# One core of block-sparse attention and a feed-forward: the written order of all engines replaced by another search's order

## The chip, the cores and the metric

The program runs on one core of one Trainium2 chip. The metric is device time in microseconds (us). The kernel before takes 261.37 us, the median of 3 runs (261.06 to 262.38).

A core has engines that run side by side, each through its own list of instructions in order: TensorE (PE in the profile; its weight loads are PEld), VectorE (DVE), ScalarE (ACT), GpSimd (POOL) and SyncE (SP), which here only starts transfers. An engine waits at an instruction until semaphores tell it that the data are there and the buffer is free. So the order in which each list is written decides who stands behind whom.

## The reference, cut to what matters

```python
# attention: batch 4, 8 heads, 768 positions, head_dim 64, blocks of 32
scores = scale * np.matmul(q, k.transpose(0, 1, 3, 2))
mask = np.abs(blk_i - blk_j) <= 1
mask = mask | (blk_i == 0) | (blk_j == 0) | (blk_i == n_blocks - 1) | (blk_j == n_blocks - 1)
# ... and three sampled key blocks for each block of queries
scores = np.where(mask, scores, -1000000000.0)
attn = softmax(scores)                 # row maximum taken off, exp, divided by the sum
x = np.matmul(attn, v)                 # to (3072 tokens, 512)
# feed-forward: 512 -> 2048 -> 512
h = x @ w_in
g = h * (1.0 / (1.0 + np.exp(-beta * h)))
out = g @ w_out
```

All inputs and the output are float32; the kernel multiplies in float16.

## The kernel before, in words

**Tiles.** Two heads of one batch make a pair; there are 16 pairs (x = 0 to 15). For each pair, keys and queries are loaded (`st`), cast to float16 (`s16`), transposed to `kX` and `qX` (the buffers `set`), and the values are cast into `va`. For the first four pairs the transposes run on TensorE (`turn`) with a copy out of PSUM behind each (`turn cp`); for later pairs they are transfers from SyncE's queue. A pair is worked in two tiles of queries, 256 and 512 wide.

**One attention tile.** Six scoring steps (`sc`, TensorE, into a double bank of PSUM), six exponentials (`ex`, ScalarE, out `et`), six multiplications by the mask (`mk`, VectorE), then the product with the values (`av`, TensorE, one step per head), the reciprocal of the sums and the scaling (`norm`, VectorE, out `xst`), and a transpose into `x`: on TensorE with a copy (`x turn`, `x cp`) for the first tiles, afterwards as a transfer (`x<-xst`). For the first six tiles the mask is not multiplied: TensorE adds it to the scores with a second product (`onehot`), so these `sc` are twice as long and there is no `mk`.

**The feed-forward.** Over groups of 256 or 512 tokens: `hp` (x by w_in, TensorE), `th` (tanh, ScalarE), `gm` (VectorE), then the product with w_out: plain (`op`) for the first group, and for the others a scheme of seven half-size products (`pr`) with sums of `g` (`sg`) and of `w_out` (`tw`) on VectorE. `cv` takes the product out of PSUM into `osb`, on ScalarE or VectorE; `osb` is then stored.

**Row tiles.** `sc` uses 64 of the array's 128 rows per product, so two heads run side by side. Some 128-row steps are written in halves and paired ("`118P1:119`" says that step 118 and step 119 alternate, half by half; `in_halves`), so that they can stand beside `sc` without a change between 64 and 128 rows.

**The order.** The steps are numbered 0 to 1298 by the order in which the program creates them. The string `STEPS` (line 43 on) holds the order of emission and all placements: `31S4` is step 31 on SP with buffer slot 4; letters P, A, D, G, S are TensorE, ScalarE, VectorE, GpSimd and SyncE. `in_steps` (line 164) reads it and sets each step's engine and slots; the loop at the end of the kernel function emits the steps in that order. Each engine's list is the subsequence with its letter. A cast on GpSimd also waits for the VectorE step emitted last before it (line 1056, "beside PSUM readers"). The loads of the first keys of pairs 1 and 0 (steps 27 and 13) are issued at the very start from ScalarE's queue, whatever their place in the string.

**Steps that the prediction names.**

| steps | what |
|---|---|
| 27, 35, 28, 36, 29, 37, 30, 38 | keys of pair 1 (first third, rest): loads, casts, turns, copies |
| 31, 32, 33, 34 | queries of pair 1: load, cast, turn, copy |
| 0, 1, 2, 3; 4 to 9 | the mask: block table, product, the shut form, its copy; three products with three copies (4 and 5, 6 and 7, 8 and 9) |
| 13 to 24 | keys and queries of pair 0 (14, 18, 22 casts; 15, 19, 23 turns; 16, 20, 24 copies) |
| 41 to 48 | keys and queries of pair 2 (42, 46 casts; 43, 47 turns; 44, 48 copies) |
| 26, 40, 50, 60 | casts of the values of pairs 0, 1, 2, 3 |
| 51 to 58 | keys and queries of pair 3 |
| 88, 92, 90; 80, 76, 78; 104, 100, 102 | first scoring steps of pairs 1, 0 and 2 |
| 94 | the first step of product with the values |
| 70 to 72, 73 to 75 | loads of w_in and w_out on GpSimd's queue |
| 172 to 181 | first group's product with w_out (`op`); 175 and 181 are its last quarters |
| 340 to 347 | sums of w_out (`tw`) |
| 480, 705, 894 | transposes of x by transfer, the last of their group; 481, 706, 930, 906 the `hp` behind them |

Of the kernel before, what the change touches and what calls it, by code (L numbers as in the profile page):

```python
# [47 lines left out]
112P1 103A6 26D1 49S6 94P0 95P 113A7 82P2 83P 96D1 97D1 116P0 84Da 185A0 114P1 117Ac 190P3 66D0  # L48
85D0 191A8 59S7 60G2 50D0 106P2 107P 108Da 109D2 115Ab 188P0 86P6 67P7 189Ad 87D1 68D 186P2
118P1:119 202P3 119P 187A9 194P0 120Dh 121D3 203A1 192P2 11P2 110P3 98P6 122P7 12D 111D 193A4  # L50
195A2 204P1 123D 99D 205A3 124P5 145P4 125A2 139P7 142P0 133P6 146A0 143A3 134A1 136P2 127P1 140A5
130P3 126D0 147D 212P2 137A6 128A2 131A4 144D 135D 141D 213A5 138D 132D 206P3 207A6 151P2 157P3
163P4 154P5 158A0 164A1 129D 155A4 152A5 159D 210P3 196P0 211Ae 165D 156D 153D 208P2 228P1 197P
209Aa 198D0 220S4 221D5 199D3 169P6 229A7 166P7 223S8 170A0 160P4 148P5 167A6 161A3 149A2 234P1
# [6 lines left out]
390P1 393P3 310P4 394A5 292P1 391A8 293A0 313P7 295P0 314A2 343D 389D 386D 346D 311A4 296A3 395D
347D 392D 301P5 302A6 298P6 405G3 227G3 412P1 294D0 315D 312D 303D 299A5 325P17:307 418P2 410S5
413A0 300D 398D 297D 307P 415P1 408G0 288G5 289S 411G1 291G2 383D 419A2 308A5 309D 326A6 327D
304P6 305A1 316P0 416A3 317A2 319P7 320A0 306D 414D 318D 417D 321D 334P5 335A1 421P1 422A7 328P1
329A6 322P0 323A0 427P3 336D 348D0 330D 324D 331P23:337 428Ab 424P2 425A1 337P 400P0:399 435P3
399P 429D 420D 426D 423D 438P2 338A1 332A5 401D8 402D0 436A4 441P3 439Ae 333D 430P0:431 440D 339D
447P2 431P 442Ac 448Aa 437D 444P3 450P1 445A0 357P4 406S2 409S 470P3 354P5:358 451A1 464P1 471A5
358P 432D9 433D3 351D 458P0 461P3 465A8 467P1 459Ad 468A2 446D 452D 355P 449D 462A6 352D 443D 349D
453P0 454P 568P1 466D 356D0 359D 473P3 455Dc 456D1 569A9 365P:362 565P0 469D 474A3 472D 570D 460D
463D 475D 576P1 566Ae 362P 363P:366 577Aa 403S2 177S 590S4 593S1 591G2 601P3 562P0 602A7 366P 361D  # L70
477P1:476 364D 604P3 476P 360D 353D 563Ab 367A1 598P0 478D3 479D2 371P 605A0 350D 582P3 599A8
583A2 623P1 368P:372 624A6 620P0 626P3 372P 579P1 369P 596S5 434S 612S2 615S8 618S7 634S6 621A1
637S0 457S 640S3 578D 594D0 613D4 584D 567D 373D 592S0 480S 580A5 627A4 481P0 482A6 499P1 564D
625D 370D 638G5 616G6 635G2 487P2 500A0 595S 571P3 572P 488A1 483D1 501D 642P0 489D 614S2 656S4
659S1 374P3:490 484P24:496 600D 573D4 636S1 657G4 660G3 643A9 617S 658S3 639S 377S 661S 378S 645P0
646Ac 490P 491A5 606D 574D0 575S1 622D 644D 619D3 492D 581D 648P3 496P 649A3 485A1 486D 508P0
509A5 510D 493P1 520P3 497A6 521A0 494A2 375P 376A 502P0 628D 503A3 522D 498D 495D 504D 603D 529D0
670P1 664P3 671Ad 511P5 512A1 517P4 513D 607P1 608P 597G2 665Ab 666D 609D1 610D3 647D 518A6 681P0
682Ae 678P3 526P5 683D 585P1 586P 587D5 588D4 505P0 527A3 679A8 692P1 519D 528D 667P3 506A4 514P1
693A0 629P2 523P2 630P 515A0 507D 650D 516D 631D0 632D0 651P0:652 668A7 684P3 524A5 525D 652P  # L80
653Dc 685Aa 641G0 532D 654D2 790P2 791A1 535P23:538 698P3 796P0 538P 539P:536 802P2 672D 686D 530D
533D 797A6 699A2 536P 803A5 537A0 669D 680D 695P0 787P3 540D 673P2 674P 675Dc 676D1 543P 696Ac
788A7 810P2 799P0 662S2 688P3:687 546P:544 800Ab 663G1 798D 694D 531D 700D 633S 380S 379S 833S6
836S4 839S8 687P 813P0 689Df 690D0 544P 811Ad 841P2 847P3 814A4 655S 534D 589S 864S0 793P0 834G0
842A9 545A 547P 848A3 677S 691S 611S 697D 701P2 702P 542D 794A0 548A1 815D 703D0 704D2 549P 550P
801D 865D5 541D 551D 705S 844P3 825P0 822P2 823A8 826Aa 845Ae 552P 553P 555P 706P0 709P1 812D 795D
792D 789D 804D 554D 837G3 707A1 710A3 708D0 711D 730P3 819P2 731A2 806P3:805 824D 732D 843D 820A2
816P0 817Ac 805P 853P2 739P3:556 872P0 807D4 808D3 867S0 870S1 895S3 898S6 866S0 849D 818D 850P3
868G1 901S7 821D 556P 854A0 715P45:712 557D 851A5 740A3 856P3 873A1 857A6 871G2 896G2 741D 852D
874D 712P 716A2 717D 827D 713A1 835S2 558S 561S 721P23:727 878P0 875P3 879A7 727P 724P4 828P0 855D  # L90
714D 876Ab 722A6 858D 899G6 560S 838S 897S1 559S 809S0 900S 869S 728A3 725A4 742P5 751P7 718P6
743A0 877D 723D 829P 726D 729D 744D 830D1 881P1 831D2 719A5 752A3 745P45:733 846D 753D 882A2 884P0
733P 885A4 734A2 746A0 720D 736P23:748 987P0 754D0 735D 747D 988A8 748P 737A3 860P3:859 738D 749A6
984P0 887P2 859P 888Aa 750D 996P1 861D7 883D 862D0 760P45:763 985Ac 1038P0 990P3 763P 764P:761
997A5 991A0 886D 757D 880D 755D 889D 759D 1039Ad 1027P1 761P 890P0:891 1018P3 1028A3 762A1 758D
765D 891P 892D6 1019A9 893D1 768P:771 1021P1 993P3 1022A6 994Ae 1015P0 771P 772P:769 1007S1 1010S5
832S 1016A1 1030P1 999P3 863S 1000A2 1031A4 902G3 840D0 766D 1011D3 769P 894S 930P1 903P7 931A2
933P3 915P0 909P2 904A1 770A 756D 767D 998D 986D 1008D6 924P6 934A5 910A4 1009S3 1013S5 1012S
1001D 989D 995D 1017D 905D1 918P7 774P 932D 773A0 921P1 935D 1032D 911D 916A2 925A0 919A3 912P3
917D 992D 920D 775P 776D 926D 906P2 777P 922A6 923D 913A0 907A1 914D 908D 1014D1 1029D 1003P3:1002  # L100
1061P0 1062A7 780P:778 1047P1 1002P 1041P0 1004Dg 1005D0 778P 1048Aa 1166P1 1050P3 1042Ae 1167A0
1024P0 781P 936P2 1025Ac 1051A2 927P0 937A6 1040D 928A4 782A 779D 951D0 1020D 953D 1023D 952D
1043D 938D 948P7 942P6 949A2 943A5 929D 1026D 785S 786S 939P3 940A3 945P2 946A1 944D 950D 947D
941D 1044P2 1034P0:1033 1053P3 1033P 1035Da 1036D1 784S 1006S2 783S 1037S 1045Ab 1054A8 1076P2
1049D 957P23:960 1077A5 1064P3 1067P0 1052D 1065A9 1068A1 960P 961P:958 1055D 1046D 954D 955D
1073P2 958P 1180P3 1070P0 1074A3 959A1 1169P2 1069D 963D 1075D 962D 1066D 956D 965P 966P 1170A4
1071A6 1056P2 1057P 1072D 1208P0 1181Ac 1058Df 967A 968P:971 1059D0 1209Ae 1078D 1200P2 1201A2
1182D 1168D 1171D 1063D 1183P3 971P 972P:969 1184Aa 1060S 1194P0 1172P2 1173Ab 969P 1080P3:1079
1211P2 970A0 1210D 1185D 964D 973D 1195A8 1079P 1212Ad 1081D9 1082D4 977P:974 1213D 1214P0 1215A1
1186P2 1197P3 1187A6 974P 978P 1083P0 975P 1198A3 1084A 1216D 1217P2 1218P 979A 1188D 1219D3  # L110
1220D2 1115P2 1189P3 1091P0 1174D 1175P2 1176P 1190P 1085P1 1116A6 1086A3 976D 1202D 1199D 1177D7
1178D0 1196D 1097P3 1191Dc 1087D1 1127P4 1094P5 1192D4 1112P1 1128A3 1092A4 1129D 1095A0 1113A5
1093D 1117D 1114D 1203P3 1204P 1124P4 1125A5 1088P2 1205Dh 1206D3 1089A4 1103P7 1118P0 1221P6
1098A6 1104A2 1119A1 1126D 1090D 1096D 1099D 1105D 1121P4 1109P1 1122A0 1110A4 1106P2 1107A2 982S
1179S1 980S 1123D 1120D 981S 1193S 983S 1130P5 1131A3 1222D 1111D 1132D 1207S 1108D 1247P6 1100P7
# [979 lines left out]
```

## Time and profile before

| what | value |
|---|---|
| median of 3 runs | 261.37 us (261.06 to 262.38) |
| the profiled execution's own time | 261.5 us |
| its span, first to last instruction | 259.7 us |
| TensorE busy | 252.3 us, 97% |
| VectorE busy | 220.1 us, 85% |
| ScalarE busy | 212.5 us, 82% |
| GpSimd busy | 37.8 us, 15% |

The profiled execution takes 1.8 us more than its span, for what lies before the first and after the last instruction. It is 0.13 us over the median of the runs. A helper records nearly all operations, so their line is L199 for almost everything; groups are told apart by what they write and read (`sc<-qX,kX` is a scoring step, `sc<-va,et` the product with the values, `sc<-x,w_in_sb` is `hp`). "64*128 64x512" is a product on 64 rows of the array with 512 columns moved. Times at the left of a timeline are us from the span's start; "x4" merges four instructions of one kind that follow each other.

### The profile page before, as it was taken

What the parts mean: (1) busy time and instruction counts of PE and PEld (TensorE: products, weight loads), DVE (VectorE), ACT (ScalarE), POOL (GpSimd) and SP (SyncE); (2) the same over time, 40 slices, a digit from 0 to 9 for tenths busy, and PEclk for the clock granted to TensorE, in tenths of its full rate; (3) what the DMA queues carried; (4) which work ended last, traced back from release to release, by engine and by line L of the source; (5) the groups of instructions that cost most, each with busy time, mean ns of one, the idle gap of its engine ahead of it and who ended that gap; (6) DMA issues with size and microseconds to landing.
All of it is one profiled execution on the core that took longest, in us unless ns stands there. A gap on an engine that the chain in (4) does not pass through costs nothing.

```text
span 259.7 us, 8901 instructions
## 1 busy us (share of the span) xinstructions
PE 252.3 (97%) x3823; PEld 171.9 (66%) x3823; DVE 220.1 (85%) x430; ACT 212.5 (82%) x287; POOL 37.8 (15%) x52
## 2 busy tenths in 40 slices
PE   5999999999999999999999999999999999999995
PEld 1576675554367866558776457846758986568884
DVE  4465548999999999999999999998999967889572
ACT  3599999899999997999988989885999892866051
POOL 4661000133400106011201410010000000000000
PEclk9999999999999999999999999999999999999999
DMA  6999999694429997734949785232051101400042
GB/s 194 371 280 225 243 190 223 222 238 129 91 70 263 285 144 194 182 62 142 237 121 257 215 120 144 25 55 67 5 175 31 23 5 53 143 0 3 0 162 83
DMA packets 49883, 36.83 MB, mean 142 GB/s; under 512 B 29732, under 2 KB 46388, under 8 KB 49844
## 3 DMA queue, kind: packets, MB, share of 16 engines
q1 hardware_dynamic: 45584, 31.80, 49.1%
q0 software_dynamic: 3680, 4.19, 9.4%
q8 instruction: 30, 0.49, 0.7%
q10 hardware_dynamic: 580, 0.26, 0.4%
q14 instruction: 9, 0.07, 0.1%
HBM read 27.27 MB, written 6.29 MB: 129 GB/s over the span
## 4 chain that ended last, share of the span: by engine, by line
PE 78%; DVE 16%; ACT 2%; DMA 2%; issue 1%; ACTq 0%; DVEq 0%
PE sc L199 78%; DVE et L199 7%; DVE g L199 5%; DMA st<-in_k_dram 2%; DVE w_mix L199 1%; ACT et L199 1%; ACT t_sb L199 1%; DVE xst L199 1%; DVE w_out_sb L199 0%; DVE s L199 0%; DVE osb L199 0%; DVE x L199 0%; DVE recip L199 0%; ACTq L362 0%; DVEq L199 0%
## 5 line engine op out<-in xcount | busy, mean ns | idle before, releaser
L199 ACT ACTIVATE et<-sc 128x1024 f16<-128x1024 f32 x144 | 139.0, 1037 | 12.6 <-PE sc L199 11.6
L199 PE MATMUL sc<-x,w_in_sb 128*128 128x512 f16 (+2 forms) x512 | 91.9, 352 | 0.1
L199 ACT ACTIVATE t_sb<-sc,beta_c_sb 128x512 f16<-128x512 f32 (+1 forms) x112 | 65.0, 646 | 20.5 <-PE sc L199 17.2
L199 DVE TENSOR_TENSOR et<-et,mask 128x960 f16<-128x960 f16 x120 | 77.5, 679 | 1.3 <-ACT et L199 1.3
L199 DVE SCALAR_TENSOR_TENSOR g<-t_sb,sc 128x512 f16<-128x512 f16 (+1 forms) x112 | 63.5, 604 | 10.0 <-ACT t_sb L199 9.8
L199 PEld LDWEIGHTS <-w_in_sb 128*128 128x128 f16 (+1 forms) x512 | 43.0, 97 | 36.3 <-issue 3.5
L199 PEld LDWEIGHTS <-g 64*128 64x128 f16 (+1 forms) x700 | 49.0, 96 | 15.0 <-issue 2.6
L199 PE MATMUL sc<-w_out_sb,g 64*128 64x256 f16 (+3 forms) x568 | 55.5, 281 | 0.0
L199 PE MATMUL sc<-qX,kX 64*128 64x512 f16 (+1 forms) x384 | 51.0, 329 | 0.6 <-ACT et L199 0.3
L199 PEld LDWEIGHTS <-et 64*128 64x128 f16 (+1 forms) x1800 | 41.4, 95 | 9.4 <-issue 2.3
L199 PE MATMUL sc<-va,et 64*128 64x65 f16 (+1 forms) x1800 | 44.5, 191 | 0.1
L199 POOL CAST s<-st 128x768 f16<-128x768 f32 (+2 forms) x19 | 18.1, 967 | 83.3 <-DVE et L199 60.3
L199 PEld LDWEIGHTS <-kX 64*128 64x128 f16 x384 | 20.1, 96 | 10.3 <-issue 5.5
L199 PEld LDWEIGHTS <-s 64*128 64x128 f16 (+1 forms) x320 | 21.8, 98 | 6.9 <-DVE s L199 2.0
L199 PE MATMUL sc<-w_mix,s 64*128 64x256 f16 (+1 forms) x272 | 23.7, 270 | 0.0
L199 ACT COPY osb<-sc 128x512 f32<-128x512 f32 (+3 forms) x23 | 12.4, 539 | 8.3 <-PE sc L199 7.3
L199 DVE TENSOR_TENSOR xst<-sc,recip 128x256 f16<-128x256 f32 (+1 forms) x32 | 17.8, 556 | 0.9
L199 DVE TENSOR_TENSOR osb<-osb,sc 128x512 f32<-128x512 f32 (+2 forms) x19 | 11.7, 616 | 7.0 <-PE sc L199 2.7
L199 PE MATMUL sc<-w_mix,g 64*128 64x256 f16 (+3 forms) x128 | 15.3, 264 | 0.0
L199 POOL CAST va<-st 128x768 f16<-128x768 f32 x9 | 8.6, 962 | 39.5 <-PE sc L199 33.0
L199 DVE RECIPROCAL recip<-sc 128x4 f32<-128x4 f32 (+1 forms) x32 | 6.1, 191 | 8.2 <-PE sc L199 7.9
L199 PE MATMUL sc<-s,onehot 64*128 64x256 f16 (+1 forms) x72 | 11.7, 338 | 0.2
(61 smaller groups left out, 95.6 us busy)
## 6 DMA issues: line engine op xcount, KB each, us to landing
out_dram<-osb SPq DMA_DIRECT2D x23, 256.0 KB, 2.4
st<-in_k_dram SPq DMA_DIRECT2D x12, 384.0 KB, 5.0
st<-in_q_dram SPq DMA_DIRECT2D x12, 384.0 KB, 4.8
st<-in_v_dram SPq DMA_DIRECT2D x12, 384.0 KB, 4.6
g<-in_v_dram SPq DMA_DIRECT2D x4, 384.0 KB, 6.5
w_in_sb<-in_moe_w_in_dram POOLq DMA_DIRECT2D x2, 512.0 KB, 8.1
w_in_sb<-in_moe_w_in_dram POOLq DMA_DIRECT2D x1, 1024.0 KB, 14.5
w_out_sb<-in_moe_w_out_dram POOLq DMA_DIRECT2D x2, 512.0 KB, 18.4
```

The source lines that it names most:

```text
L199: r = f(*a, **kw)
```

## The change

Only the string `STEPS` differs. The same 1299 steps are in it, with the same instructions; their order of emission, the slots, and the engine of 22 steps are others. The order was found by a search over a model of the chip's engines in which TensorE was given a wait at every 256th instruction; nothing of that wait is in the program.

Counted from the two strings: TensorE has 433 steps in both, and most of them move by a place or two (at most 25), in neighbouring pairs that change places; its list is rearranged more in its first 20 steps and from step 1083 to 1265. ScalarE has 286 and 282 steps, VectorE 417 and 417, GpSimd 39 and 43, SyncE 124 and 124. Both have 44 pairs by halves (written with a colon); 651 with 652 are paired only before, 175 with 181 only after. The list of TensorE changes between 64-row and 128-row steps 68 times before and 64 times after; two of the four that go are among the first 25 steps, the other two at steps 175 and 181.

Steps whose engine changes (in order of time):

| step | kind | before | after |
|---|---|---|---|
| 34, 48 | `turn cp` | ACT | DVE |
| 38 | `turn cp` | DVE | ACT |
| 7 | mask copy | DVE | ACT |
| 46 | cast (queries, pair 2) | POOL | DVE |
| 14, 26, 50, 224 | casts | DVE | POOL |
| 619, 840, 1011, 1014 | casts | DVE | POOL |
| 834, 871, 902 | casts | POOL | DVE |
| 537, 770, 782, 970, 979 | `cv` | ACT | DVE |
| 1149 | `cv` | DVE | ACT |

The diff, cut to the first lines and to the place of 175 and 181:

```diff
 STEPS = """
-31S4 0D 1P0 27S0 35S 32D0 33P4 28D1 45S1 13S1 29P7 17S3 21S 46G6 36D 18G2 30D0 3A 4P5 8P1 2A 41S0
-6P0 7D 61S 42G3 51S2 62G5 37P3 52G4 55S3 34A 88P3 89Ab 69G 70G 38D 14D0 92P1 93A0 9D 47P1 15P0
-19P4 22D 23P6 5A 16D2 24D 20D 71G 72G 73G 74G 75G 90P1 80P2 43P6 44D1 48A 91A2 76P1 10S 65S 63P0
-64D 104P3 81A1 77A3 105A4 53P1 78P1 56D3 57P4 54D3 58D 79Ae 39S5 25S4 100P0 40D3 184P3 102P2 101A5
...
+27S0 0D 1P2 3A 4P7 5A 13S1 14G5 35S 6P0 8P1 2A 28D3 31S4 36D 37P6 32D1 17S3 18G2 61S 45S1 21S 29P4
+33P2 19P3 15P5 9D 30D0 34D 38A 7A 92P3 41S0 93A1 42G4 62G0 51S2 55S3 52G6 88P0 25S4 10S 39S5 46D3
+16D1 20D 22D 23P2 90P2 24D 80P1 43P6 47P7 89A0 69G 70G 49S6 71G 72G 26G1 91Aa 76P0 63P4 59S7 65S
+73G 50G0 60G2 44D3 48D 81A2 77A8 64D 56D1 74G 75G 104P3 105A3 78P2 53P2 57P3 100P0 79Ac 101Ae 54D2
...
-271A2 264Aa 173P 174P:180 345D 222S0 237P0 275P2 238A5 180P 266P3 175P 181P 265D 239D 271D 226S2
...
-268D 279P0:278 247P 340D 341D 342D 256G6 387P2 248De 249D1 290S0 404S3 285G4 259G0 257S 286S3 183S
...
+240P3 260P0 241A1 233D 261Aa 236D 245D 242D 178P 272P2 262D 273A0 179P:173 263P3 269P0 340D 344D
+341D 270A6 264A5 173P 174P:180 271D 237P2 238Ac 275P0 180P 266P3 274D 265D 226S5 222S0 225S 252S1
+181P:175 276A2 239D 345D 277D 253G4 387P2 396P0 175P 267A3 268D 246P3:247 397A8 176A1 279P0:278
...
```

More of the change, by code (lines that the diff above doesn't have):

```diff
@@ L49 @@
[L49 to L54, printed above, removed]
@@ L61 @@
[L61 to L66, printed above, removed]
@@ L67 @@
[L67 to L108, printed above, removed]
@@ new lines @@
+604P3 563Ab 476P 367A0 360D 598P0 361D 364D 353D 605A3 599A2 371P 478D2 479D3 623P3 624A4 582P1
+350D 368P:372 593S3 596S4 612S2 615S7 620P0 603D 570D 594D5 583Aa 613D6 403S2 618S5 434S 457S
+634S1 616G3 626P3 372P 579P1 369P 621Ad 580A0 627A8 373D 592S0 637S6 635G1 480S 481P4 482A3 499P2
+500A0 487P3 488A4 564D 370D 567D 625D 571P3 572P 483D1 501D 595S 642P0 643A5 614S3 377S 636S1
+640S2 656S8 659S0 662S7 573D8 489D 574D0 575S0 374P4:490 484P23:496 581D 644D 584D 606D 638G4 628D
+645P0 648P3 617S 490P 646A1 491A6 492D 578D 657G6 660G5 639S 658S2 661S 378S 496P 508P0 497A5
@@ new lines @@
+1003P3:1002 1062A5 780P:778 1047P1 1048Ae 1002P 1041P0 1004Da 1005D4 778P 1166P1 1050P3 1042Ad
+779D 1040D 1032D 1024P0 1025A1 781P 783S 784S 1051A2 1167Ab 936P5 937A3 1026D 927P0 928A1 942P1
+948P6 943A4 949A0 782D 1020D 938D 929D 944D 939P3 940A5 945P2 946A6 1049D 950D 941D 947D 954D
+1044P2 1034P0:1033 1053P3 1033P 1035Df 1036D0 1045A9 1043D 1054A3 952D 1076P2 957P23:960 1077A0
+1064P3 1067P0 960P 961P:958 1073P2 1068A4 1065A1 958P 1055D 955D 1052D 1078D 1046D 1168D 1180P3
+1070P0 1074A7 959A1 1169P2 962D 1170A6 1171D 965P 966P 1071A8 967A 1181Aa 1056P2 1057P 1069D
@@ new lines @@
+1013S5 964D 956D 1058D8 1059D2 1063D 1072D 1208P0 968P:971 1209A2 1183P3 1200P2 1201A3 971P
+972P:969 1075D 1066D 1014G2 963D 785S 786S 1194P0 1172P2 1184A9 1173Ac 969P 1080P3:1079 1211P2
+970D0 973D 1079P 1210D 1081D0 1082D1 1195Ad 1212Ae 1214P0 977P:974 1215A1 1186P2 1197P3 974P
+1187A0 1198A4 1182D 1174D 1196D 1188D 1175P0 1176P 1177Dd 975P 1006S1 1037S 1060S 1083P5 1084A
+978P 1216D 1213D 1217P2 1115P6 1202D 1178D4 976D 1218P 1185D 1199D 1219Dc 1220D1 1085P3 1116A3
+1086A6 979D 1087D1 1117D 1097P0 1189P2 1190P 1094P2 1098A6 1095A4 1099D 1191D6 1203P3 1204P 1205Dg
@@ new lines @@
+1192D3 1091P3 1092A2 1093D 1112P4 1113A5 1114D 1103P0 1221P1 1096D 1206D2 1179S2 1088P3 1089A2
+1130P4 1131A5 1222D 1104A1 1090D 1132D 1109P7 1110A3 1111D 1105D 1124P3 1127P2 1125A0 1128A4 1207S
+980S 1193S 981S 983S 982S 1118P1 1121P0 1129D 1126D 1122A6 1119A2 1106P6 1100P7 1107A0 1101A1
+1123D 1120D 1108D 1102D 1253P2 1259P4 1235P1 1223P3 1224A4 1133D0 1225D0 1241P6 1260A6 1268P5
+1242A3 1136D 1139P7 1142P0 1135D 1243D 1140P 1247P3 1143P 1269A4 1236A3 1137D 1270D 1134D 1141A0
+1254A1 1232P5 1147P 1250P6 1237D 1145D 1144D 1261D 1138D 1148P 1150P 1149A 1151P 1153P 1154P
@@ L124 @@
+1229P1 1152A1 1251A6 1233A4 1255D 1146D 1256P4 1230A1 1248A5 1249D 1155D 1231D 1265P2 1156P 1157P
+1257A2 1258D 1262P3 1226P1 1238P4 1263A5 1227A3 1266A0 1158D 1234D 1252D 1264D 1267D 1228D 1244P5
+1245A1 1246D 1239A5 1240D 1271D0 1274D 1272D 1273D 1163S 1162S 1159P 1275D 1160P 1161A 1277P6
+1278A0 1279P3 1280D 1276D 1282D 1281D 1283P 1284A 1164S 1165S 1285P 1287P 1286A1 1289P 1288D 1297S
+1290D 1291A 1292P 1293A 1296S 1294P0 1295D 1298S
 """
```

65 lines of the change are left out of this document (44 added, 21 removed).

## The prediction

> **What bounds the kernel now.** I read the page's first part, the chain that ended last, and then busy time by stages.
>
> ```profile
> span 259.7 us, 8901 instructions
> PE 252.3 (97%) x3823; PEld 171.9 (66%) x3823; DVE 220.1 (85%) x430; ACT 212.5 (82%) x287; POOL 37.8 (15%) x52
> ```
> ```profile
> PE 78%; DVE 16%; ACT 2%; DMA 2%; issue 1%; ACTq 0%; DVEq 0%
> ```
> ```profile
> 0.00:13.00 13.00, 10.01 (x65) 4.89 (x66) 5.85 (x26) 6.26 (x9) 6.77 (x20) 1.00 0.87 283
> 13.00:33.00 20.00, 19.91 (x302) 13.92 (x301) 11.76 (x31) 20.00 (x28) 5.48 (x7) 1.00 1.17 248
> 42.00:75.00 33.00, 32.44 (x504) 16.48 (x502) 32.69 (x57) 31.51 (x43) 9.10 (x10) 1.00 0.62 158
> 160.00:240.00 80.00, 79.98 (x1216) 57.60 (x1211) 71.48 (x131) 62.43 (x88) 0.87 (x1) 1.00 0.19 49
> ```
> ```profile
> 120.00:160.00 40.00, 39.66 (x654) 26.51 (x651) 38.18 (x68) 36.31 (x47) 7.32 (x8) 1.00 0.85 195
> ```
>
> The columns of a stretch are its length, then busy time of PE, PEld, DVE, ACT, POOL, then clock and transfers. TensorE carries 78% of the chain and stands still almost only in the first 13 us (3.0 us there, 0.56 us in 42 to 75, 0.02 us in 160 to 240). An order can therefore win only in three places: the start, small stops and mode changes inside TensorE's busy time, and stretches where another engine paces it: ScalarE at 13 to 33 (20.00 of 20), VectorE at 42 to 75 (32.69 of 33). The same products remain, so nothing near the 16% of VectorE in the chain is on offer.
>
> **Start.** The timeline of the first 13 us:
>
> ```profile
> 1.43 0.92 ACTq L509 DMA_DIRECT2D st<-in_k_dram  x2
> 5.36 0.63 DVE L199 CAST s<-st 128x256 f16<-128x256 f32 x2 [1.69 <-DMA st<-in_k_dram]
> 6.03 1.14 PE L199 MATMUL sc<-mask_q,onehot 24*128 24x384 f16 x3
> 6.93 0.82 POOL L199 CAST s<-g 128x768 f16<-128x768 f32 x1 [3.22 <-DMA g<-in_q_dram]
> 7.64 0.40 PE L199 MATMUL sc<-s,onehot 64*128 64x256 f16 x2
> 9.46 1.67 PE L199 MATMUL sc<-identity,s 128*128 128x128 f16 x14
> 11.47 0.42 PE L199 MATMUL sc<-s,onehot 64*128 64x256 f16 x2
> 11.68 0.42 PE L199 MATMUL sc<-qX,kX 64*128 64x256 f16 x2
> 12.14 5.68 ACT L199 ACTIVATE et<-sc 128x1024 f16<-128x1024 f32 x6 [0.41 <-PE sc L199]
> 13.31 0.28 PE L199 MATMUL sc<-s,onehot 64*128 64x256 f16 x2
> ```
> ```profile
> 17.68 0.27 PE L199 MATMUL sc<-s,onehot 64*128 64x256 f16 x2
> 17.79 0.27 PE L199 MATMUL sc<-qX,kX 64*128 64x256 f16 x2
> 18.00 1.49 PE L199 MATMUL sc<-va,et 128*128 128x65 f16 x41
> ```
> ```profile
> L199 DVE CAST s<-st 128x256 f16<-128x256 f32 x3 | 0.8, 283 | 1.7 <-DMA st<-in_k_dram 1.7
> L199 DVE CAST mask<-sc 128x384 f16<-128x384 f32 x2 | 1.1, 554 | 0.8 <-PE sc L199 0.8
> L199 DVE COPY kX<-sc 128x256 f16<-128x256 f16 x2 | 0.6, 292 | 1.5 <-PE sc L199 1.5
> L199 DVE COPY kX<-sc 128x512 f16<-128x512 f16 x2 | 0.8, 424 | 0.4 <-PE sc L199 0.4
> L199 DVE COPY qX<-sc 128x768 f16<-128x768 f16 x1 | 0.6, 558 | 0.4 <-PE sc L199 0.4
> ```
>
> The gate is the key load of pair 1 on ScalarE's queue: VectorE casts at 5.36, and scoring starts at 7.64. The load stays where it is, so 5.36 stays. In the new list VectorE then does casts 28 and 36 (0.63), 32 (0.283), mask copy 9 (0.554), copies 30 and 34 (0.292 each): scoring from 5.36 + 2.05 = 7.4. TensorE does its three mask products (4, 6, 8) in that wait instead of at 6.03, and turns 19 and 15 before scoring instead of among the fourteen products from 9.46. Pairs of 256-column products start every 0.21 us here (11.47, 11.68) and every 0.11 us later (17.68, 17.79): the first 13 us run at half speed. From 7.4 to step 76, which starts at 13.31 now, the new list has the scoring steps 92, 88, 90 and 80, four pairs each (16 × 0.21 = 3.4), and sixteen 128-column turns (23, 43, 47) of 1.67/14 = 0.12 (1.9): step 76 at 12.7, 0.6 to 0.7 earlier. Between there and step 94 at 18.00 two changes of row mode go: 0.2 more (price below), so −0.9.
>
> Against it: the query load of pair 2 goes from SyncE's third transfer to its fifth, the keys of pair 2 one place later; SyncE issues one each 0.51 us, so its cast, now at 6.93 on GpSimd, could start at 8.0, on VectorE ahead of copies 16 and 20 and cast 22, which turn 23 needs at 9.1. With 0.55 for cast 46 (row below), 0.29 twice and 0.42 turn 23 would wait until 9.5: +0.4, and 1 us more if both land later still. I take +0.1, nearer to the row, whose 3.22 us of waiting shows a transfer that others slow and that need not move by the full 1.0. Sum −0.8, bounds −0.9 and +0.5. ScalarE's third exponential no longer stands behind mask copy 5 and copy 48 until 12.14 (48 goes to VectorE, 7 and 38 come), so ScalarE, the pacer to 33, gains as much and keeps it.
>
> **Mode changes.** Four rows of TensorE's timeline, around steps 175 and 181:
>
> ```profile
> 47.30 0.38 PE L199 MATMUL sc<-w_out_sb,g 64*128 64x512 f16 x2
> 47.52 0.38 PE L199 MATMUL sc<-qX,kX 64*128 64x512 f16 x2
> 47.83 1.90 PE L199 MATMUL sc<-w_out_sb,g 128*128 128x512 f16 x8
> 49.66 0.52 PE L199 MATMUL sc<-va,et 64*128 64x65 f16 x22
> ```
>
> From 64-row to 64-row work the next start comes after 0.22; from 64 to 128 rows after 0.31: 0.09 to 0.10 for one change. The list has 68 of them before and 64 after. Two are in the start's sum; the two around steps 175 and 181 go with their pairing, which costs no more array time (eight products on 128 rows or sixteen halves, two at once): −0.2. The pair 651 and 652 that is undone stands beside another 128-row step, at no change in count: 0.
>
> **VectorE's and ScalarE's load.**
>
> ```profile
> L199 DVE CAST s<-st 128x768 f16<-128x768 f32 x7 | 3.7, 545 | 0.0
> L199 DVE CAST va<-st 128x768 f16<-128x768 f32 x3 | 2.3, 760 | 0.0
> L199 DVE CAST va<-g 128x768 f16<-128x768 f32 x3 | 2.0, 691 | 0.0
> L199 DVE COPY osb<-sc 128x512 f32<-128x512 f32 x4 | 2.7, 684 | 0.0
> ```
>
> Before 42 us VectorE loses casts 14, 26, 50, 224 (0.28 + 0.69 + 0.69 + 0.55), mask copy 7 (0.55) and copy 38 (0.42), and takes 46, 34, 48 (0.55, 0.29, 0.56): 1.8 us less where it is about to become the pacer. At 42 to 75 TensorE stands 0.56 us by the windows, and the chain's VectorE pieces lie there. I take −0.4 of it, most of the 0.56; bounds −0.6 and 0, since three sums of w_out (340, 344, 341) now come ahead of mask steps. From 120 to 146 VectorE gets 537, 834 and 871 (0.68 + 0.55 + 0.76 = 2.0) into a stretch with 40 − 38.18 = 1.8 us free: 0 if its lead is still there, +2.0 if not; I take 0. The later moves nearly cancel (+902, 770, 782, −840, −1011, −1014) or lie where TensorE has little need (970, 979, where 80 − 71.48 us are free). GpSimd's four added casts stand ahead of its w_out loads, 2 us later; first use is at 40.8 and later, and I price this at 0, bound +0.5.
>
> **Waits planned, not there.** The search gave TensorE a wait at every 256th instruction.
>
> ```profile
> q8 instruction: 30, 0.49, 0.7%
> ```
> ```profile
> PEld L199 <- issue: 17.7, 59, 0.6
> PE sc L199 <- DVE s L199: 1.4, 1, 1.4
> ```
>
> Thirty loads of 0.49 MB/30 = 16 KB against 7646 weight loads and products: one per 256. But the longest row of a wait of TensorE's products is this 1.4 us, for VectorE; the weight loads' 17.7 us lie beside running products, since all of TensorE's still time is 259.7 − 252.3 = 7.4 us, 3.0 of it at the start. The wait itself costs 0 in both lists. [...]
>
> **Sum.** Against the profiled execution's 261.5: −0.8 − 0.2 − 0.4 = 260.1; it stands 0.13 over the median, so 260.0. The other moves of TensorE's steps are mostly swaps of neighbours; where they go further (1083 to 1265), TensorE has no still time to gain, and VectorE and ScalarE have 8.5 and 17.6 us free in 80. I price them at 0, with ±1.0, twice the still time of 42 to 75.
>
> **Rivals.**
>
> *Slower: transposes without margin.* All `hp` of a token group wait for the last transpose of x.
>
> ```profile
> 166.73 1.19 SPq L747 DMA_TRANSPOSE x<-xst  x1
> ```
> ```profile
> 170.23 1.04 PE L199 MATMUL sc<-x,w_in_sb 128*128 128x512 f16 x4
> ```
> ```profile
> x<-xst SPq DMA_TRANSPOSE x22, 3.6
> ```
>
> From the issue of transpose 894 to its `hp` are 3.5 us, for a median landing of 3.6: no margin. Where VectorE reaches that last `norm` later against TensorE, every microsecond goes to TensorE. With VectorE's 2.0 us more from 120 to 146, the joint before 706 and this one would lose 1 to 2 us each: 260.0 + 3.0 = 263.0. Here it decides from the first tenth of lateness on. For it: 38.18 of 40 busy. Against it: VectorE's lead of 1.8 us.
>
> *No change: the start's gain is not kept.* The query and key loads that moved back land late, or VectorE's order at 42 to 75 takes it back: 261.5 − 0.2 − 0.13 = 261.2. The planned waits that do not exist speak for it: the order is made for a TensorE that comes later, so the change would not do what it says.
>
> [...]
>
> **How the numbers follow.** Forecast case 0.34 (own range 259.4 to 260.7), clock 0.12, no change 0.28, slower 0.26. Half a percent is 1.3 us, about what a measurement tells here: faster means under 260.06. Of the forecast 0.28 lies there and 0.06 within; the clock case is faster; the case of no change is within; of the slower case 0.03 stays within. So faster 0.40, within 0.37, slower 0.23. The range reaches from the clock case, 258.7 with −0.5 of swaps, to 263.2, just over the slower case.
>
> **What would show it.** First scoring at 7.4 instead of 7.64, the first product with values near 17.0 instead of 18.00; steps 175 and 181 as 64-row products without the 0.10; TensorE's still time at 42 to 75 near 0.2. Wrong: scoring after 7.6, a wait of `hp` on a transpose, or VectorE full at 120 to 160 with TensorE waiting on it.

## The result, and the profile after

The changed kernel takes **265.26 us**, the median of 4 runs (264.8 to 265.43), against 261.22 (260.81 to 262.38) for the kernel before on the same chip: a ratio of **1.0138, 95% interval 1.0112 to 1.0163**. The forecast was 260.0 with a range to 263.2. The change made the kernel slower by 1.4%, and the time lies outside the range. Ratios leave out single runs that took over 1.5% longer than the fastest of their kernel: one each in experiments 5, 6 and 12, and one of the kernel before beside experiments 1 to 4.

The page of the changed kernel, its first lines and the chain that ended last:

```profile
span 263.4 us, 8872 instructions
PE 252.0 (96%) x3807; PEld 172.6 (66%) x3807; DVE 221.4 (84%) x430; ACT 211.7 (80%) x283; POOL 41.1 (16%) x56
...
PE 77%; DVE 12%; DMA 4%; ACT 3%; issue 2%; ACTq 0%; SPq 0%; POOL 0%; DVEq 0%; POOLq 0%
PE sc L199 77%; DVE et L199 4%; DVE g L199 3%; DMA qX<-s 2%; DMA st<-in_k_dram 2%; ACT t_sb L199 2%; ACT et L199 1%; DVE xst L199 1%; DVE va L199 1%; DVE s L199 1%; DVE recip L199 1%; DVE osb L199 0%; ACTq L362 0%; DVE kX L199 0%; SPq L747 0%
```

TensorE is busy as long as before (252.0 against 252.3 us), so all of the 3.7 us of span is time in which it stands still. One entry of the chain is new, `DMA qX<-s` with 2%, and "issue" has gone from 1% to 2%. Busy time by stages, columns as in the prediction (length, PE, PEld, DVE, ACT, POOL, clock, transfers):

```profile
0.00:13.00 13.00, 9.45 (x60) 4.70 (x61) 5.65 (x25) 6.53 (x10) 5.65 (x19) 1.00 0.85 278
...
42.00:75.00 33.00, 32.45 (x510) 17.02 (x508) 31.62 (x57) 31.84 (x43) 8.63 (x9) 1.00 0.77 186
75.00:120.00 45.00, 41.99 (x678) 29.02 (x671) 41.66 (x73) 39.21 (x49) 9.67 (x9) 1.00 0.70 154
120.00:160.00 40.00, 39.93 (x606) 27.28 (x605) 38.43 (x71) 36.05 (x45) 5.56 (x6) 1.00 0.62 146
```

The one stage that stands out is 75 to 120 us: TensorE stands 3.0 us there, where it stood 0.07 us in the kernel before:

```profile
75.00:120.00 45.00, 44.93 (x760) 31.44 (x754) 43.80 (x81) 42.02 (x51) 8.22 (x8) 1.00 0.79 175
```

The waits of TensorE name two places, the timeline shows them:

```profile
PE sc L199 <- issue: 1.8, 1, 1.8
...
PE sc L199 <- DMA qX<-s: 0.9, 1, 0.9
```
```profile
75.73 0.64 PE L199 MATMUL sc<-va,et 64*128 64x65 f16 x29
78.17 0.48 PE L199 MATMUL sc<-va,et 64*128 64x65 f16 x19 [1.80 <-issue]
```
```profile
111.13 0.61 PE L199 MATMUL sc<-qX,kX 64*128 64x256 f16 x8 [0.92 <-DMA qX<-s]
```

The first is the odd one. TensorE stops in the middle of a pair of `av` steps, after 29 of 48 like products, with the same operands before and behind, and nothing that the profile knows is waited for ("issue"). From start to start the gap is 2.0 us. The second is scoring step 670, which waits for a transposing transfer.

Set step against step, the new kernel is 0.6 us late at the first products with values (step 82, 19.40 against 18.79 us), has won that back by 75 us (0.1 late), is 2.1 late behind the stop, 2.5 at 95 us, 3.4 behind step 670, and 3.6 at the end.

What ran just ahead of the stop differs: SyncE's list in the two kernels, before first, after second (start, length, what is issued).

```profile
74.69 1.19 SPq L747 DMA_TRANSPOSE x<-xst  x1
...
76.55 0.43 SPq L509 DMA_DIRECT2D st<-in_k_dram  x1
```
```profile
70.85 0.46 SPq L509 DMA_DIRECT2D st<-in_k_dram  x1
...
72.89 0.69 SPq L509 DMA_DIRECT2D st<-in_q_dram  x1
74.65 1.92 SPq L747 DMA_TRANSPOSE x<-xst  x1
```

Before, the transposing transfer of x (step 403, 74.69) stands ahead of the loads of pairs 8 and 9 (590, 593, 596, 612, 615) and holds them back until 76.55. In the new list they stand ahead of it, and leave as a burst of five times 384 KB from 70.85 on. The same windows in both, before first:

```profile
72.50:76.00 3.50, 3.05 (x126) 2.16 (x126) 3.47 (x8) 3.50 (x6) 0.00 (x0) 1.00 0.04 10
```
```profile
72.50:76.00 3.50, 3.08 (x130) 2.09 (x124) 3.41 (x8) 3.50 (x6) 0.00 (x0) 1.00 0.97 303
76.00:78.00 2.00, 0.37 (x23) 0.24 (x15) 2.00 (x4) 0.91 (x1) 0.00 (x0) 1.00 1.00 356
```

10 GB/s against 303, and then TensorE does 0.37 us of work in 2.

**The theory.** TensorE's instructions come in 16 KB loads, one per 256 instructions (the q8 row of the prediction: 30 loads, 0.49 MB, for 7646 weight loads and products; 29 loads, 0.48 MB, for 7614 in the changed kernel). In the trace the starts of these loads can be set beside the place that TensorE has reached. Count TensorE's recorded rows, weight loads and products together with the rows of its sequencer (five up to here), in the order of their starts: the stop falls on row 2241, which is 9 × 256 − 63; taking 256k − 63 as the ends of the blocks, the load for the next block mostly starts within 1.3 us of TensorE's entry into a block where few transfers run, and 2 to 3.5 us after it where many do. In the new kernel TensorE enters a block at 72.76 us; the block holds two pairs of `av` steps, which are 256 instructions in only 3.4 us; the load for the next one runs from 75.76 to 76.64, and the next instruction starts at 78.16. In the kernel before the same block is entered at 72.78, its load runs from 73.64 to 74.58, and nothing stops at 76.22. So: *the burst delays the instruction load, and a block (256 instructions) of short products is over before the next is there.* The rival: the stop belongs to the new order itself, by a dependence that the trace does not show.

### The profile page after: what moved, and what is told of

Same layout as the page of the kernel before. It is cut to its first block, busy times and chain, and to the rows that moved or that the text cites. A ratio compares the mean times of both kernels' runs of the same rounds, so it can differ in the third digit from the quotient of the medians.

```text
span 263.4 us, 8872 instructions
## 1 busy us (share of the span) xinstructions
PE 252.0 (96%) x3807; PEld 172.6 (66%) x3807; DVE 221.4 (84%) x430; ACT 211.7 (80%) x283; POOL 41.1 (16%) x56
## 4 chain that ended last, share of the span: by engine, by line
PE 77%; DVE 12%; DMA 4%; ACT 3%; issue 2%; ACTq 0%; SPq 0%; POOL 0%; DVEq 0%; POOLq 0%
PE sc L199 77%; DVE et L199 4%; DVE g L199 3%; DMA qX<-s 2%; DMA st<-in_k_dram 2%; ACT t_sb L199 2%; ACT et L199 1%; DVE xst L199 1%; DVE va L199 1%; DVE s L199 1%; DVE recip L199 1%; DVE osb L199 0%; ACTq L362 0%; DVE kX L199 0%; SPq L747 0%
## 5 line engine op out<-in xcount | busy, mean ns | idle before, releaser
L199 DVE TENSOR_TENSOR et<-et,mask 128x960 f16<-128x960 f16 x120 | 76.4, 675 | 0.9 <-ACT et L199 0.8
L199 PE MATMUL sc<-w_out_sb,g 64*128 64x256 f16 (+2 forms) x576 | 55.6, 282 | 0.3 <-DVE g L199 0.2
L199 POOL CAST s<-st 128x768 f16<-128x768 f32 (+2 forms) x21 | 20.0, 960 | 86.1 <-PE sc L199 30.9
L199 POOL CAST va<-st 128x768 f16<-128x768 f32 x10 | 9.6, 961 | 80.1 <-PE sc L199 63.6
L199 DVE TENSOR_TENSOR xst<-sc,recip 128x256 f16<-128x256 f32 (+1 forms) x32 | 17.8, 556 | 0.9
L199 ACT COPY osb<-sc 128x512 f32<-128x512 f32 (+3 forms) x19 | 9.8, 532 | 9.6 <-PE sc L199 8.6
```

The lines of the kernel that those rows point to most:

```text
L199: r = f(*a, **kw)
```

## The experiments

All ratios are to the kernel before, run on the same chip beside each kernel.

**1. The loads later.** In the new order, 403 goes ahead of the loads, and the casts that read them go later with them.

```diff
-... 576P1 590S0 411G3 463D 591G2 ... 593S3 596S4 612S2 615S7 ... 594D5 583Aa 613D6 403S2 618S5 ... 595S
+... 576P1 411G3 463D ... 583Aa 403S2 590S0 591G2 593S3 596S4 612S2 615S7 618S5 ... 594D5 613D6 595S
```

> The changed order, but SyncE issues the output transfer 403 ahead of the five 384 KB loads 590, 593, 596, 612 and 615 (and the two casts on VectorE that read them, 594 and 613, stand later). The loads then leave from about 75.9 us, as in the kernel before, and not from 70.9. Theory (TensorE's next 256 instructions are fetched too late behind the loads): the 16 KB instruction load of 75.76 comes within 1 us of 72.8, the stop of 2.0 us at 76.2 in the 64x65 products is gone, and the time falls by 2.0 to about 263.2. Rival (the stop belongs to the new order itself, with a wait that the trace does not show): the stop stays and the time stays at 265.3.

Measured: ratio 1.0356 (1.027 to 1.0443), 271.4 us: much slower than the 263.2 expected. The stop is gone, as the theory said: the instruction load ran from 73.16 to 74.34, and TensorE went on at 75.93 without a gap. The time went to another place that neither side had foreseen. TensorE's, GpSimd's, VectorE's and SyncE's rows, in this order:

```profile
99.78 2.80 PE L199 MATMUL sc<-x,w_in_sb 128*128 128x512 f16 x9 [3.76 <-DMA x<-xst]
```
```profile
93.20 1.60 POOL L199 CAST s<-st 128x768 f16<-128x768 f32 x2 [6.95 <-PE sc L199]
```
```profile
91.68 1.22 DVE L199 TENSOR_TENSOR et<-et,mask 128x960 f16<-128x960 f16 x2
```
```profile
94.05 1.48 SPq L568 DMA_TRANSPOSE kX<-s  x1
...
96.26 1.20 SPq L747 DMA_TRANSPOSE x<-xst  x1
```

Cast 591 (93.20, on GpSimd) starts just after VectorE's second mask step, 570, ends at 92.90 (the profile puts its wait down to TensorE). Cast 591 had been moved behind 570 in the string, and in this program a cast on GpSimd waits for the VectorE step emitted last before it. Transfer 592, which needs the cast, is issued at 94.05 instead of 89.70 in the changed kernel, and behind it in SyncE's list stands 480 (96.26), the transpose of x that `hp` 481 waits for. Two waits of `sc` for transposes of queries follow (1.89 us at 105.79, 1.69 us at 116.21), and the granted clock is 0.50 for 3.4 us behind the first wait; whether these come of the same cast is not shown. The experiment answers its question (the stop) and shows a price of moving a cast, 3.8 us, that has nothing to do with it.

**2. The same loads, the blocks shifted.** 96 tiny products of zeros in TensorE's idle time before 8 us move every block by 192 instructions; nothing else is touched.

```diff
-... 3A 4P7 ... 36D 37P6 ... 33P2 19P3 ...
+... 3A 14x4V5 4P7 ... 36D 12x4V5 37P6 ... 33P2 70x4V3 19P3 ...
```

> The changed order, with 96 products of 4 columns by 16 columns of zero weights (192 instructions) added to TensorE in the idle time of the first 8 us: no order, load or transfer is touched, but every block of 256 instructions begins 192 instructions earlier in the work. Theory of the late fetch: no block ends at 76.2 any more (one begins at about 73.3 and ends near 78), so the 2.0 us stop there is gone, with the burst of loads still there; and as a block of only 2.0 us now lies at 50.5 to 52.5, a new stop of 1 to 2.5 us comes at about 52.5. Time 264 to 266. Rival (the stop hangs on the burst, the order or a semaphore): the stop stays in the pair of products where it is, and none comes at 52.5; time 265.3.

Measured: ratio 1.0171 (1.0099 to 1.0243), 266.4 us, just over the 264 to 266 expected. With all loads as they were, the stop is gone from the pair of `av` steps where it stood, and a new one stands where the theory put it, in the run of `av` products near 52 us. It is 0.98 us from start to start, the lower end of what was expected:

```profile
75.75 0.93 PE L199 MATMUL sc<-va,et 64*128 64x65 f16 x48
...
76.79 0.93 PE L199 MATMUL sc<-va,et 64*128 64x65 f16 x48
...
80.38 0.39 PE L199 MATMUL sc<-qX,kX 64*128 64x512 f16 x2 [1.25 <-ACT et L199]
```
```profile
50.49 2.33 PE L199 MATMUL sc<-va,et 64*128 64x65 f16 x138
53.62 1.02 PE L199 MATMUL sc<-va,et 64*128 64x65 f16 x54 [0.79 <-issue]
```

The expectation had the block that begins near 73 end without a stop at 78. That part missed: it began at 74.33 and ended at 79.1, the load for the next block ran from 77.94 to 78.92, and TensorE stands 1.3 us there. The profile puts this gap down to ScalarE; the block's end falls on it, so the two cannot be told apart there. The rival is out: a stop that belongs to products or semaphores would not move with 192 instructions that are long over.

**3. The burst in the kernel before.**

```diff
-... 577Aa 403S2 177S 590S4 593S1 591G2 ... 596S5 434S 612S2 615S8 618S7 ...
+... 577Aa 590S4 593S1 596S5 612S2 615S8 403S2 177S 591G2 ... 434S 618S7 ...
```

> The kernel before, with the five loads 590, 593, 596, 612 and 615 issued ahead of the output transfer 403, that is from about 69.9 us instead of 76.5. Nothing else is changed. Theory of the late fetch: the block that TensorE enters at 72.8 gets its successor only about 3 us later, and a stop of 1.5 to 2 us without a semaphore comes at 76.2: time 262.8 to 263.3. Rival (the burst is harmless, the new order lost the time): no stop there, time 261.2.

Measured: ratio 1.0104 (1.0034 to 1.0174), 264.7 us, more than the 262.8 to 263.3 expected. The stop is there, in the old order:

```profile
75.11 0.77 PE L199 MATMUL sc<-va,et 64*128 64x65 f16 x37
77.85 0.36 PE L199 MATMUL sc<-va,et 64*128 64x65 f16 x11 [1.98 <-issue]
```
```profile
72.50:76.00 3.50, 2.92 (x125) 2.02 (x117) 3.47 (x8) 3.50 (x5) 0.00 (x0) 1.00 1.01 340
76.00:78.00 2.00, 0.15 (x10) 0.15 (x12) 0.34 (x1) 0.27 (x1) 0.00 (x0) 1.00 1.33 243
78.00:81.50 3.50, 3.50 (x29) 1.62 (x25) 3.02 (x6) 2.07 (x3) 0.00 (x0) 0.53 0.41 114
```

Five loads issued about 7 us earlier (the first at 69.38 instead of 76.55), and nothing else moved, cost the old kernel 1%. The last row shows a second price: TensorE's granted clock is 0.53 on average in the 3.5 us behind the stop.

**4. Transfer 617 earlier.**

```diff
-... 614S3 377S 636S1 640S2 656S8 659S0 662S7 ... 575S ... 617S
+... 614S3 617S 377S 636S1 640S2 656S8 659S0 662S7 ... 575S
```

> The changed order, with the transposing transfer 617 (queries of pair 9) issued right behind 614, at about 99.7 us instead of 105.5. Theory (scoring step 670 waited 0.98 us for 617 alone): the wait at 109.8 us is gone and TensorE gains 0.9 to 1.0 us there, kept to the end: 264.3. Rival (the next thing is late as well, the keys of that pair or ScalarE's tiles): less than 0.3 us, 265.1.

Measured: ratio 1.0158 (1.0104 to 1.0213), no gain where 264.3 us was expected. The wait of step 670 is gone:

```profile
110.79 0.61 PE L199 MATMUL sc<-qX,kX 64*128 64x256 f16 x8
```

But in this kernel's profile the stop is 2.8 us long instead of 2.0, and the clock falls behind it:

```profile
77.36 0.48 PE L199 MATMUL sc<-va,et 64*128 64x65 f16 x19 [2.62 <-issue]
```
```profile
75.00:77.50 2.50, 0.14 (x9) 0.14 (x11) 1.50 (x3) 0.28 (x1) 0.00 (x0) 1.00 1.53 342
77.50:81.00 3.50, 3.50 (x37) 1.76 (x34) 2.49 (x5) 2.06 (x3) 0.00 (x0) 0.56 0.87 165
```

The mean granted clock is 0.990 to 0.994 in all four runs of this kernel, where it is 0.998 to 1.0 in the four of the changed one, so the fall is no accident of one profile. While the stop is there, it hides what a microsecond elsewhere is worth.

**5 and 6. Step 403 alone ahead of the loads; then 617 too.** The cure without the moved casts.

```diff
-... 576P1 590S0 411G3 ... 613D6 403S2 618S5 ...
+... 576P1 403S2 590S0 411G3 ... 613D6 618S5 ...
```

> The changed order with one step moved: SyncE issues the output transfer 403 ahead of load 590, so that the burst of five loads leaves from about 75.6 us again; all casts stay where the changed list has them. Theory of the late fetch: the fetch of 75.76 comes at about 73.3, the stop at 76.2 is gone as it was with the loads behind 403, and the 3.9 us wait of first-layer step 481 that came there (its transposing transfer 480 stood behind 592, whose cast on GpSimd had been moved) does not come. Time 263.3, with nothing under full clock after the first microseconds. Rival (loads that leave 5 us later are missed by the steps of pair 8 and 9, whatever the casts): the stop is gone but a wait on those transfers takes its place, 264.5 or more.

> The kernel with 403 first, and 617 issued right behind 614 as well. If both faults are separate, they add: stop of 2.0 us and wait of 0.98 us gone, 262.3. If something behind them ends at the same time (VectorE's tiles at 94, the mode change), only one of the two is won: 263.3.

Measured: 403 first, ratio **1.0043** (1.0026 to 1.006); with 617 early as well, 1.0032 (1.0016 to 1.0048). Moving one transfer past its neighbours takes back 0.95%, 2.5 us of the loss. No wait for 480 came, though the loads leave as late as in experiment 1 (75.19 against 75.64 us). So the rival of this run falls, and the 3.8 us of experiment 1 come of the casts that were moved there. The place of the stop:

```profile
75.01 0.93 PE L199 MATMUL sc<-va,et 64*128 64x65 f16 x48
75.78 0.59 PE L199 MATMUL sc<-qX,kX 64*128 64x512 f16 x4
```
```profile
72.50:76.00 3.50, 3.07 (x134) 2.17 (x126) 3.40 (x7) 3.50 (x5) 0.00 (x0) 1.00 0.21 42
```

617 is worth 0.1% in the ratios, with intervals that overlap. In the two profiles, a wait of 1.09 us at 108.6 goes with it, and what lies behind comes 1.2 us earlier.

**7 to 11. Pieces of both orders.** The first 187 steps (to about 36 us) are the same set in both strings, and but for two steps so are the first 440 (to about 82 us). So the strings can be cut there and put together, with buffers renamed where they meet.

7, the old start before the repaired new order, and 8, the new middle alone:

> The first 187 steps (to about 36 us) are those of the kernel before, the rest is the changed order with 403 first and 617 early; slots are renamed so that both fit. If the new start costs what the two first profiles show (0.6 us at the first product of probabilities and values), this is 0.5 to 0.6 faster than the kernel with both repairs: 261.8. If the start differs only by when the first loads land in a run (this product came between 17.3 and 19.4 us in four profiles that have one and the same start), it is the same: 262.3.

> Steps 1 to 187 from the kernel before, 188 to 440 (about 36 to 82 us of VectorE's and TensorE's work) from the changed order, the rest from the kernel before, which has 403 ahead of the loads. If the middle stage of the new order is worth the 0.45 us that it won back between 42 and 75 us, 260.8, 0.5 under the kernel before. If that gain hangs on being late at 42 us (it only caught up), 261.3.

The old start before the repaired new order: ratio 1.0033 (1.002 to 1.0045), the same as without it. Its profile has a wait of 1.22 us for another transposing transfer, at 111.4 us.

The old start, the new middle and the old rest: 1.0181 (1.0167 to 1.0195), a miss by 5 us. The cause stood in the buffers: load 596 was given one whose last reader, cast 411, came late, SyncE stood at it from 76.9 to 83.8, and `hp` 481 waited 3.07 us for its transpose again:

```profile
76.45 0.47 SPq L509 DMA_DIRECT2D st<-in_q_dram  x1
83.78 0.37 SPq L509 DMA_DIRECT2D st<-in_v_dram  x1
```
```profile
99.22 1.01 PE L199 MATMUL sc<-x,w_in_sb 128*128 128x512 f16 x2 [3.07 <-DMA x<-xst]
```

The remedy is one slot (596 in 3, the later 640 in 8):

```diff
-... 596S8 434S 612S2 615S5 618S7 634S6 637S0 640S3 ...
+... 596S3 434S 612S2 615S5 618S7 634S6 637S0 640S8 ...
```

9 is 8 with that slot, 10 the new start and middle before the old rest, 11 the new start alone:

> As the last kernel (steps 1 to 187 and from 441 on from the kernel before, 188 to 440 from the changed order), but load 596 gets a staging buffer that has long been free (3 instead of 8, whose reader, cast 411, came late: 596 left at 83.8 us there and step 481 waited 3.2 us for its transfer behind it). Theory: that wait was the whole loss, 592 is issued before 90 us again, and what is left is the middle of the new order: 260.8 (0.998 of the kernel before) if its 0.45 us is real, 261.5 if it only catches up a late start. Rival (the middle of the new order leaves VectorE or a queue late for the stages behind it): over 262.5.

> Steps 1 to 440 from the changed order, the rest from the kernel before, load 596 in the same free buffer. It holds the new start and the new middle, but neither the stop at 76.2 nor the wait for 617. If the loss lies wholly behind step 440, as the common steps of the two first profiles say (0.09 us apart at 75.4 us): 261.5 or 1.000 of the kernel before. If the new start costs 0.6 us of its own: 262.1 or 1.0025.

> Steps 1 to 187 from the changed order, the rest from the kernel before. The start alone, the other way round than the kernel that had both repairs and the old start: 262.1 (1.0025) if the new start costs 0.6 us, 261.5 (1.000) if it costs nothing, 260.7 (0.997) if it saves the 0.8 us that the prediction gave it.

| kernel | steps to 187 | 188 to 440 | from 441 | ratio | interval |
|---|---|---|---|---|---|
| changed | new | new | new | 1.0138 | 1.0112 to 1.0163 |
| with 403 and 617 repaired | new | new | new, repaired | 1.0032 | 1.0016 to 1.0048 |
| the same, old start (7) | old | new | new, repaired | 1.0033 | 1.002 to 1.0045 |
| 10 | new | new | old | 0.9991 | 0.9972 to 1.001 |
| 11 | new | old | old | 1.0048 | 1.0023 to 1.0074 |
| **9** | old | new | old | **0.9960** | 0.9945 to 0.9975 |

Number 9 is faster than both kernels: 260.66 us, median of 12 runs (260.27 to 261.01), where the kernel before takes 261.49. Its page:

```profile
span 258.6 us, 8924 instructions
...
PE 89%; DVE 6%; ACT 2%; DMA 1%; issue 1%; ACTq 0%; DVEq 0%
```

So the middle of the new order is a gain (0.4%, 1.05 us), and the loss lies behind step 440: 265.26 becomes 261.3 when only that part is the old one again. The start is harder to tell. New against old start costs nothing in front of the repaired rest, 0.3% in front of the old rest with the new middle (10 against 9), 0.5% with the old middle (11). In the profile of 11 there are gaps of 0.5 and 0.6 us at ends of blocks (76.2 and 89.7 us), where the kernel before has none and 0.2 us, so at least a part of its 0.5% is not the start itself.

**12. A shift by 24 instructions.**

```diff
-... 33P2 19P3 ...
+... 33P2 12x4V3 19P3 ...
```

> The changed order with 12 small products (24 instructions) added in the idle time of the first 8 us: every block of 256 instructions begins 24 instructions earlier in the work, the loads are as they were. Theory of the late fetch: the stop is still there, as the block is still short and the burst falls on it, but it stands 24 instructions earlier in the pairs of 64x65 products (after about 17 instead of 29 products of the pair's run), and as it ends when the instructions come, it is longer by the 0.25 us that these take: 2.0 to 2.5 us, time 265.3 to 267 (the upper end if the clock falls behind the stop, as it did behind those of 2.1 us and more). Rival (the stop hangs on a product, a buffer or a semaphore): same products before and after it as in the changed kernel.

Measured: ratio 1.016 (1.0117 to 1.0202), and the sharpest row of the study:

```profile
75.19 0.45 PE L199 MATMUL sc<-va,et 64*128 64x65 f16 x17
76.74 0.67 PE L199 MATMUL sc<-va,et 64*128 64x65 f16 x31 [1.10 <-issue]
```

17 products ahead of the stop and 31 behind it, where there were 29 and 19: exactly 24 instructions earlier. Its length missed: 1.3 us between starts, not 2.0 to 2.5. The block was entered earlier (71.78), and the load for the next one ran from 74.43, after 2.65 us and not 3.0. A gap of 2.0 us ahead of step 670, for which the profile names VectorE, took the place of the wait for 617 in this run; its cause is open.

The instruction loads of the blocks in question, read from the trace's transfers (us):

```
kernel              block entered  load of the next   next starts  start to start of the stop
before                  72.78        73.64 - 74.58       76.22       none
changed                 72.76        75.76 - 76.64       78.16       1.98
loads later (1)         72.49        73.16 - 74.34       75.93       none
403 first (5)           72.04        72.53 - 73.76       75.47       none
before, burst (3)       72.25        75.54 - 76.41       77.85       2.16
617 early (4)           71.13        74.99 - 76.01       77.36       2.80
shift by 24 (12)        71.78        74.43 - 75.39       76.73       1.28
shift by 192 (2)        50.62        51.24 - 52.37       53.62       0.98
```

In each kernel that stopped, the next block starts 1.25 to 1.52 us after its load has ended. The last row needs no burst: its block is so short (2.0 us by the work in it) that even a load started after 0.6 us is late.

## Why the prediction was wrong

**The step that failed is "Waits planned, not there": "the wait itself costs 0 in both lists".** It cost 2.0 us in the new list, and 2.5 us (1.0138 to 1.0043) by the run that takes it away. The reasoning went from the profile of before, where one instruction load per 256 instructions was seen and no stop, to the new list, as if the absence were a property of the kernel. It was a margin. The block entered at 72.78 us lasted 3.44 us, and the load for the next block was over 1.64 us before its end, where 1.25 to 1.52 us lie between the two in the stopped kernels. The kernel before even has a small stop: its block that ends at 89.27 us had its successor loaded from 86.80 to 87.86, and the 48 `av` products at that end take 0.98 us to the next product's start, where the next 48 take 0.76. The change moves the loads 590 to 615 past 403 in SyncE's list; the text priced SyncE's moves at the start alone and never asked what else those transfers share. Blocks of 256 instructions whose successor is loaded while they run (0.49 to 3.86 us after they were entered, in the table above) agree with the stops of the runs here. Weighed as a rival, a load that comes too late would have asked which block is shortest and what runs beside it.

Of the 1.38%, 0.95 go when 403 is moved, 0.11 with 617, and 0.41 when the list behind step 440 is the old one (1.0032 against 0.9991); the new start and middle before the old rest are 0.09 under the kernel before, within its interval.

**The second term that was missing is 617** (0.92 us of waiting in the first profile). The rule by which the text looked for trouble, "transposes without margin", was the right kind: a transposing transfer issued late with its reader close behind. But it was applied to the transposes of x before `hp` 706 and 930, which show no such wait, and not to those of queries and keys. Its price in the time is unsure, as the ratios of the repairs differ by 0.1% only.

**"Start", −0.8: wrong.** Scoring began at 8.56 us, not at 7.4, and the first product with values at 18.63, not near 17.0:

```profile
4.74 0.83 DVE L199 CAST s<-st 128x256 f16<-128x256 f32 x3 [1.47 <-DMA st<-in_k_dram]
...
8.78 0.56 DVE L199 CAST s<-g 128x768 f16<-128x768 f32 x1 [1.92 <-DMA g<-in_q_dram]
```
```profile
8.02 0.61 PE L199 MATMUL sc<-identity,s 128*128 128x128 f16 x4 [1.56 <-POOL s L199]
8.56 0.40 PE L199 MATMUL sc<-s,onehot 64*128 64x256 f16 x2
```
```profile
7.22 0.74 POOL L199 CAST s<-st 128x256 f16<-128x256 f32 x2 [3.70 <-DMA st<-in_k_dram]
```

The gate that was assumed, the cast of the keys of pair 1 at 5.36, came at 4.74, and it did not matter. Turn 19 now stands ahead of scoring, and it waits for cast 18, which stands behind cast 14 on GpSimd and the load for that (7.22). The text moved 19 and 15 forward and took them as filling; they brought their own load's time with them. The bound against it, cast 46 holding VectorE, was seen rightly (1.92 us of waiting). The hybrids put the start between 0 (7) and +0.8 us (10 against 9), and 11 at +1.25 us with some of it not the start. How early the first loads land differs between profiles: step 82 came between 17.3 and 19.4 us in nine kernels that have the new start, and between 17.8 and 18.8 in five that have the old one, so a single profile does not measure a start to half a microsecond.

**"VectorE's and ScalarE's load", −0.4: not borne out, though the time came.** VectorE's busy time at 42 to 75 fell from 32.69 to 31.62 us, as it was meant to. But TensorE's still time there, which was to go from 0.56 to near 0.2, is 0.55 in the changed kernel and in kernel 9: no gain of VectorE's free time shows. What the middle wins comes at another place, the steps 175 and 181:

```profile
48.02 0.38 PE L199 MATMUL sc<-qX,kX 64*128 64x512 f16 x2
48.24 1.03 PE L199 MATMUL sc<-w_out_sb,g 64*128 64x512 f16 x8
49.10 0.59 PE L199 MATMUL sc<-qX,kX 64*128 64x512 f16 x4
49.53 1.03 PE L199 MATMUL sc<-w_out_sb,g 64*128 64x512 f16 x8
```

From the first of these rows to the scoring product behind the next 192 `av` products, the new order takes 5.40 us (48.02 to 53.42), the old one 5.81 for the same work (47.52 to 53.33). Of these 0.41 us, 0.21 are scoring and the quarters 175 and 181 as halves, **"Mode changes", −0.2: right**; 0.20 come because the `av` products run unbroken (3.03 us, against 3.23 with scoring steps among them), which the text left at 0 with the other moves. Kernel 9 shows the same 5.40 us. By the ratios it wins 1.05 us (0.65 to 1.4); in its profile 0.57 of 1.08 us are there at the first product with values already, where the order is still the same, so what of the gain beyond 0.4 us belongs to the middle is open.

**The rivals.** "No change: the start's gain is not kept" had the start right and the end wrong. The clock case, which sets the low end of the range (258.7), uses a term that no run shows; in its place the changed kernel's trace shows pairs of 256-column products that start every 0.21 us up to 12.38 us and every 0.11 from 13.57 on (11.68 and 13.31 in the kernel before), and step 76 began at 13.57 us, later than before. "Slower: transposes without margin" named the wrong joints (617, above). The "other moves of TensorE's steps" were priced at 0 with ±1.0; the list behind step 440, repaired, costs about 1.1 us (1.0032 against 0.9991). All engines' lists differ there, and no run separates which of the moves cost it. The text's reading that TensorE stands still almost only in the first 13 us also left out 3.2 of the 7.4 us, which lie behind 240 us; the result does not hang on it.

## What to carry to other kernels

When a trace shows a resource with a margin, compute the margin; that no stop is seen says nothing of the next order. Where TensorE runs hundreds of short products in a few microseconds, look at what else is being transferred then: here one transfer moved in front of five bulk loads held them until the dense block was over, and took the ratio from 1.0138 to 1.0043. An order's loss can often be located in a few runs by cutting both orders where the same steps are done and joining the halves, but each joint needs its buffers and its casts' waits looked at first: a moved cast and a shared buffer cost 3 to 4 us each here by one late reader (waits of 3.76 and 3.07 us).

## What the runs showed of the hardware that was not expected

**Instruction loads came late among data transfers.** The load of TensorE's next 16 KB of instructions began 0.4 to 1.1 us after the block at 72 us was entered in eight of the nine kernels without the burst (10 to 48 GB/s at 72.5 to 76), and 2.65 to 3.9 us after it in the four with the burst (303 to 359 GB/s). Transfers of data are not all of it: in the ninth, number 11, none runs between 72.3 and 73.8, yet the load began after 1.5 us, and TensorE stood 0.47 us at the block's end. What makes it wait was not tried.

**A stop of just over 2 us cost the clock too.** In the profiles with stops of 0.98, 1.28 and 1.98 us the granted clock stayed at 1.00; behind stops of 2.16 and 2.80 us, and behind waits of 3.1 and 3.8 us for a transfer, it fell to 0.50 for 3.41 us, which costs some 1.7 us more (an estimate: half of the 3.41; eight 128-row products of 256 columns took 1.89 us behind the stop of experiment 4, and 1.05 in experiment 12). Length alone does not decide: a wait of 2.03 us in experiment 12 and one of 1.89 in experiment 1 left the clock at 1.00, where an idle time of 1.98 us in experiment 3 took it down. In the kernel before and the changed one the trace's records of the clock begin at 12.78 and 12.89 us with 1.00, and the fall at the end comes 72 and 73 times 3.41 us later (at 258.54 and 262.07). Cut into such windows from there, the two traces show the fall behind a window in which TensorE was busy for 1.39 and 1.48 us, and none behind windows with 1.96 us or more; the windows ahead of the falls in experiments 1, 3, 4 and 8 held 0.41 to 1.43 us. No run tested this.
